# Blocks of 420 and 248 columns in a fused attention and gated MLP kernel

## The chip, the cores and the metric

The kernel runs on one core of a Trainium2 chip. The metric is the device time of one execution in microseconds (us). A core has TensorE (PE, matrix multiplies; PEld are its weight loads, which overlap with it), VectorE (DVE), ScalarE (ACT), GpSimd (POOL) and SyncE (SP), which here issues nearly all DMAs. SBUF is the memory that the engines work on, in 128 partitions; PSUM takes the results of matmuls.

## The reference

Batch 4, 4 heads, 1088 positions, head width 32. First a linear attention with products of two sketches as features, then a gated MLP whose gate mixes positions with a 1088 x 1088 matrix.

```python
def phi(x):                                   # 8 x 8 = 64 features
    a = einsum('rd,bhsd->bhsr', S1, x); b = einsum('rd,bhsd->bhsr', S2, x)
    return einsum('bhsi,bhsj->bhsij', a, b).reshape(..., 64)
kv = einsum('bhsf,bhsd->bhfd', phi(k), v); z = sum(phi(k), axis=2)
x = (einsum(phi(q), kv) / (einsum(phi(q), z) + 1e-6))      # heads side by side: 128 wide
h = gelu_tanh(x @ w_in)                       # 1024 wide
u, v = h[..., :512], h[..., 512:]
v_n = (v - mean(v)) / sqrt(var(v) + 1e-6) * g_ln
v_s = einsum('ts,bsd->btd', w_sg, v_n) + b_sg
out = x + (u * v_s) @ w_out
```

## The kernel before

**Words.** The large matmuls run in a fast fp32 form that keeps fewer bits of its operands. So each operand is split into a high and a low word (`x_h`, `x_l`, `w_h`, `w_l`, `ar[e][:, 0]` and `ar[e][:, 1]`), and a product is three matmuls: high by high, low by high, high by low. The high word is made by a cast on ScalarE, the low one by a subtraction on VectorE (or GpSimd).

**The mixing of positions** takes nearly all of the time. `w` (the transpose of w_sg) has 1088 rows, in 8 tiles of 128 and one of 64, and 1088 columns, in the three blocks of `CH`: 362, 362 and 364. v_n has 512 columns, in 4 blocks `db` of 128. One output block (db, ci) is 128 x the width of block ci.

Batch 0 computes each output block directly: 8 row tiles times three matmuls (`group`), and two more for the last tile (`tail`). For db 2 and 3 that is `standard`, for db 0 and 1 the loops near L1218 and `z0`.

Batches 1 to 3 call `pair` twice each, for db 0 and 1 (turn) and for db 2 and 3. Within `pair` the first two column blocks and the two halves of the rows (tiles 0 to 3 and 4 to 7) are a 2 x 2 matrix, which multiplies the 2 x 2 matrix of two db and two halves in the seven-product form: `product` is one of seven, 4 tiles times three matmuls of HW*2 = 362 columns. The third column block is computed plainly by `whole`. `unit` makes the u of one block (three matmuls, a Gelu on ScalarE), `evac` moves a product from PSUM and adds, `gate` multiplies by u, splits the result into words and adds its part of the output projection (three matmuls) to `po`. So the number of matmuls does not depend on the widths in `CH`.

**Combinations of w.** The seven products need sums and differences of the quarters of w. `combine` makes them once, while batch 0 is in its `standard` blocks: per row tile t (4) and half h of a block (2) it loads four pieces of w into `tmp`, forms four combinations on VectorE (three to DRAM tile `td` as words "1", "3", "2"; the fourth stays in SBUF as `t4`, three of eight slots in `t4a` and five in `t4b`). `stream` later writes one of "1", "2", "3" or the original "b" over the middle block of `w_h` and `w_l`, four times two in each batch, between products that read the old and the new words.

**Attention of the next batch** is woven between these blocks (`attention`): k1 (sketches of k, 9 matmuls), `features`, k2 (with v in `vx`, 9 tiles), kv and its words `kvt`; then for three chunks `CA` of q: q2, a round over DRAM (`dq`) that spreads the sketches into `ea` and `eb`, their product, its words in `r0` and `eb`, q3, and the division. Then v1, Gelu, LayerNorm (squares go to `waste`, a view of `kpt[2]`).

**The order** is a list written out by hand of a search, `ORDER`: one number for each step in the order in which `add` and `step` made them. Each engine runs its steps in that order, and SP is one queue for loads, stores and streams. `keep` are 12 matmuls without use that stand in the start, and 14 small ones run before the first data come (`WARM`).

**The end.** The last block is done by `finish` in two halves: scale and gate on VectorE, one fp32 matmul, addition, store.

Of the kernel before, what the change touches and what calls it, by code (L numbers as in the profile page):

```python
# [1341 lines left out]
```

## Time and profile before

| What | Value |
|---|---|
| time, median of 3 runs | 335.23 us (334.34 to 335.45) |
| the profiled execution's own time | 335.34 us |
| its span, first to last instruction | 333.2 us |
| TensorE busy | 326.9 us (98%), 2000 matmuls |
| VectorE busy | 264.8 us (79%) |
| ScalarE busy | 219.4 us (66%) |
| GpSimd busy | 54.0 us (16%) |
| DMA | 52.5 MB, 158 GB/s on average |
[...]

The span is what the profiler sees; some 2 us of the time lie around it. Durations of matmuls overlap, since one starts before the one before it has left the array, so that distances between starts tell more than durations. Idle time of an engine is time that it waits; what released it stands behind an arrow.

### The profile page before, as it was taken

To read this page: it belongs to the slowest core of one execution; us is meant where nothing else is said; L and a number is where in the kernel's file an instruction comes from. 1 tells how busy PE (TensorE), PEld (TensorE's weight loads), DVE (VectorE), ACT (ScalarE), POOL (GpSimd) and SP (SyncE) were. 2 spreads that over 40 slices of the span, in tenths; PEclk is the share of its full clock that TensorE was granted. 3 is DMA by queue.
4 is the path that set the end of the run, shared out by engine and by line. 5 is a ranking of instruction groups with operands and counts; after the bars stand their busy time and mean duration, and the time that the engine had idled before them with its cause. 6 is when DMAs were issued, how large, how long until landed. Compare 5 with 4: busy or idle time off the path is not lost.

```text
span 333.2 us, 5905 instructions
## 1 busy us (share of the span) xinstructions
PE 326.9 (98%) x2000; PEld 319.2 (96%) x2000; DVE 264.8 (79%) x603; ACT 219.4 (66%) x533; POOL 54.0 (16%) x123
## 2 busy tenths in 40 slices
PE   7999999999999999999999999999999999999995
PEld 7998899999999999999999999999999999999994
DVE  3899989999996879899786588989864595986564
ACT  6578885576899977546888964566889743233321
POOL 1695781000003300000003200000015100000000
PEclk9999999999999999999999999999999999999999
DMA  7979455656656476964458115660073038004701
GB/s 236 376 258 327 135 167 148 188 168 179 183 171 205 134 229 197 290 186 110 115 165 270 37 48 174 205 191 0 22 220 117 3 106 247 27 22 124 256 9 60
DMA packets 43854, 52.54 MB, mean 158 GB/s; under 512 B 3952, under 2 KB 41136, under 8 KB 43824
## 3 DMA queue, kind: packets, MB, share of 16 engines
q1 hardware_dynamic: 43680, 52.08, 51.0%
q8 instruction: 15, 0.25, 0.3%
q14 instruction: 15, 0.12, 0.1%
q10 hardware_dynamic: 144, 0.09, 0.1%
HBM read 43.17 MB, written 8.99 MB: 157 GB/s over the span
## 4 chain that ended last, share of the span: by engine, by line
PE 96%; DMA 1%; SPq 1%; DVE 1%; issue 0%; DVEq 0%
PE pz L830 16%; PE pz L832 16%; PE pz L831 15%; PE ps L928 4%; PE ps L747 2%; PE ps L746 2%; PE ps L745 2%; PE po L784 2%; PE po L783 2%; PE po L782 2%; PE pz L842 2%; PE pz L841 2%; PE ps L1010 2%; PE ps L920 2%; PE ps L1011 2%; PE ps L1012 2%
## 5 line engine op out<-in xcount | busy, mean ns | idle before, releaser
L830 PE MATMUL pz<-w_h,ar 128*128 128x362 f32 (+1 forms) x288 | 95.6, 332 | 0.0
L832 PE MATMUL pz<-w_l,ar 128*128 128x362 f32 (+1 forms) x288 | 94.6, 328 | 0.0
L831 PE MATMUL pz<-w_h,ar 128*128 128x362 f32 (+1 forms) x288 | 94.3, 327 | 0.0
L830 PEld LDWEIGHTS pz<-w_h,ar 128*128 128x128 f32 x288 | 54.2, 188 | 0.7
L831 PEld LDWEIGHTS pz<-w_h,ar 128*128 128x128 f32 x288 | 54.3, 188 | 0.5
L832 PEld LDWEIGHTS pz<-w_l,ar 128*128 128x128 f32 x288 | 54.2, 188 | 0.0
L776 ACT CAST gh<-gt 128x362 fp32r<-128x362 f32 (+1 forms) x47 | 22.8, 494 | 28.0 <-PE po L783 15.2
L805 ACT CAST ar<-vn 128x512 fp32r<-128x512 f32 x40 | 24.3, 618 | 17.0 <-PE pz L832 14.4
L777 DVE TENSOR_TENSOR gl<-gt,gh 128x362 fp32r<-128x362 f32 (+1 forms) x47 | 24.5, 530 | 10.3 <-ACT gh L776 9.9
L307 POOL TENSOR_TENSOR st<-st 128x4 f32<-128x4 f32 (+2 forms) x8 | 2.8, 346 | 177.7 <-DVE st L289 177.7
L806 DVE TENSOR_TENSOR ar<-vn,ar 128x512 fp32r<-128x512 f32 x40 | 27.3, 684 | 4.7 <-ACT ar L805 4.6
L751 ACT ACTIVATE u<-ps 128x362 f32<-128x362 f32 (+1 forms) x48 | 22.1, 469 | 13.0 <-PE ps L747 8.6
L324 ACT ACTIVATE vn<-vn,st 128x512 f32<-128x512 f32 x33 | 25.7, 812 | 1.7 <-POOL st L318 1.4
L775 DVE TENSOR_TENSOR gt<-gt,u 128x362 f32<-128x362 f32 (+1 forms) x47 | 24.6, 528 | 1.5 <-ACT u L751 1.2
L699 POOL TENSOR_TENSOR w_l<-w_f,w_h 128x362 fp32r<-128x362 f32 (+1 forms) x21 | 21.6, 1063 | 2.9 <-ACT w_h L652 2.6
L761 DVE SCALAR_TENSOR_TENSOR gt<-pz,g_col,b_bc 128x362 f32<-128x362 f32 (+1 forms) x31 | 18.2, 587 | 2.1 <-PE pz L842 2.1
L1022 ACT ACTIVATE kp<-vn,st 128x512 bf16<-128x512 f32 x27 | 19.4, 718 | 0.2
L1019 ACT ACTIVATE vn<-ps 128x512 f32<-128x512 f32 x27 | 16.0, 593 | 4.2 <-PE ps L1012 4.1
L782 PE MATMUL po<-gh,wout_h 128*128 128x362 f32 (+1 forms) x47 | 15.9, 339 | 0.0
L745 PE MATMUL ps<-x_h,win_h 128*128 128x362 f32 (+1 forms) x48 | 15.9, 331 | 0.0
L747 PE MATMUL ps<-x_l,win_h 128*128 128x362 f32 (+1 forms) x48 | 15.8, 329 | 0.0
L746 PE MATMUL ps<-x_h,win_l 128*128 128x362 f32 (+1 forms) x48 | 15.8, 328 | 0.0
(299 smaller groups left out, 805.3 us busy)
## 6 DMA issues: line engine op xcount, KB each, us to landing
w_l<-td SPq DMA_DIRECT2D x52, 181.0 KB, 4.6
w_h<-td SPq DMA_DIRECT2D x26, 362.0 KB, 4.4
w_f<-in_w SPq DMA_DIRECT2D x9, 544.0 KB, 6.0
tmp<-in_w SPq DMA_DIRECT2D x16, 181.0 KB, 3.4
vx<-in_v SPq DMA_DIRECT2D x8, 288.0 KB, 6.6
ea<-dq SPq DMA_DIRECT2D x12, 182.0 KB
eb<-dq SPq DMA_DIRECT2D x12, 182.0 KB, 2.9
td<-tmp SPq DMA_DIRECT2D x8, 271.5 KB
```

The lines of the kernel that those rows point to most:

```text
L324: A.activation(self.vn(t), self.vn(t), AF.Identity, bias=self.nm[:, t : t + 1], scale=self.rs[:, t : t + 1])
L745: mm(o, lhsT=win_h[:, ws], rhs=xh[:, cs], start=True, stop=False)
L746: mm(o, lhsT=win_l[:, ws], rhs=xh[:, cs], start=False, stop=False)
L775: add("V", dv(cw), lambda: V.tensor_mul(gt(k)[:, :cw], gt(k)[:, :cw], utt[plan.got[u]][:, :cw]), r=[u], w=[k], free=[u], port=1)
L776: add("A", ac(cw), lambda: A.copy(ght[plan.got[h]][:, :cw], gt(k)[:, :cw]), r=[k], take={h: "gh"})
L777: add("V", dv(cw), lambda: V.tensor_sub(glt[plan.got[l]][:, :cw], gt(k)[:, :cw], f32(ght[plan.got[h]][:, :cw])), r=[h, k], take={l: "gl"}, ...
L782: mm(o, lhsT=wout_h[:, db], rhs=hh, start=i == 1, stop=False, skip_group_check=True)
L805: add("A", ac(n), lambda: A.copy(dst[:, 0], q()), r=r, w=[key])
L806: add("V", dv(n), lambda: V.tensor_sub(dst[:, 1], q(), f32(dst[:, 0])), r=r, w=[key], port=1)
L830: mm(o, lhsT=ar[e][:, 0, t], rhs=wh, start=first, stop=False, skip_group_check=True)
L831: mm(o, lhsT=ar[e][:, 1, t], rhs=wh, start=False, stop=False, skip_group_check=True)
L832: mm(o, lhsT=ar[e][:, 0, t], rhs=wl, start=False, stop=last, skip_group_check=True)
```

## The change

- The column blocks `CH` are 420, 420 and 248 wide, `HW` is 210. Tiles that hold a block (`gt`, `u`, `gh`, `gl`) are 420 wide, `td` and the slots of `t4` too: two in `t4a`, six in `t4b`. The chunks `CA` of the attention stay.
- v of batch 0 lies in a staging tile, v of batches 1 to 3 in `ea` (first half) and `eb` (second), with a memset of its ones on GpSimd before each load. The words of kv lie in the tiles of `kp1` and `kp2`, which are made anew where they are needed; `waste` is a view of `kp0`.
- `combine` loads three times in place of two and holds the four pieces in another order, so that the three combinations that go to DRAM lie side by side: one cast for two, one subtraction for two, two stores for three.
- In the end the sums of x lie in `r0`, `ea` and `r2`.
- `ORDER` is new: 1963 steps in place of 1972.

```diff
-CH = [(0, 362), (362, 362), (724, 364)]
+CH = [(0, 420), (420, 420), (840, 248)]
-HW = 181
+HW = 210
 ORDER = [
...
 ]
-    vx = const([P, 2 * NT + 1, 64], "vx")
-    G.memset(vx[:, NT], 1.0)
...
-    kvt = [const([P, 2 * P], f"kv{i}", F32R) for i in "hl"]
...
-    waste = kpt[2].bitcast(mybir.dt.bfloat16)
+    waste = kp0.bitcast(mybir.dt.bfloat16)
...
+    vx = staged("vx", [P, 2 * NT + 1, 64], "vx")
+    step("vx1", "G", 0.1, lambda: G.memset(vx()[:, NT], 1.0))
...
-        return [t4a[0][:, 362 * i : 362 * i + 362] if i < 3 else t4b[:, i - 3] for i in (2 * t, 2 * t + 1)]
+        return [t4a[0][:, 420 * i : 420 * i + 420] if i < 2 else t4b[:, i - 2] for i in (2 * t, 2 * t + 1)]
...
+                load_(0.62, lambda t=t, c=c, s=s: load(s[:, :2], wd[:, t, : 4 * HW].rearrange("p (a c) -> p a c", a=2)[:, :, c : c + HW]), w=k[:2])
                 for i in range(2):
-                    load_(0.53, lambda t=t, i=i, c=c, s=s: load(
-                        s[:, 2 * i : 2 * i + 2], wd[:, t + 4 * i, : 4 * HW].rearrange("p (a c) -> p a c", a=2)[:, :, c : c + HW]),
-                        w=k[2 * i : 2 * i + 2])
+                    load_(0.33, lambda t=t, i=i, s=s, wp=wp: load(s[:, 2 + i], wp(t + 4, 1 - i)), w=k[2 + i : 3 + i])
...
-                add("A", ac(2 * HW), lambda s=s, hi=hi: A.copy(hi[:, :2], s[:, :2]), r=k[:2], w=hk[:2])
-                add("A", ac(HW), lambda s=s, hi=hi: A.copy(hi[:, 2], s[:, 3]), r=[k[3]], w=[hk[2]])
...
-                add("V", dv(2 * HW), port=1, f=lambda s=s, hi=hi: V.tensor_sub(f32r(s[:, :2]), s[:, :2], f32(hi[:, :2])), w=k[:2], r=hk[:2])
-                add("V", d, port=1, f=lambda s=s, hi=hi: V.tensor_sub(f32r(s[:, 3]), s[:, 3], f32(hi[:, 2])), w=[k[3]], r=[hk[2]])
...
-                load_(1.14, lambda t=t, c=c, hi=hi: load(td[:3, t, 0, :, c : c + HW].rearrange(by), f32(hi)), r=hk, w=nk[:3])
-                load_(0.8, lambda t=t, c=c, s=s: load(td[:2, t, 1, :, c : c + HW].rearrange(by), s[:, :2]), r=k[:2], w=nk[3:5])
-                load_(0.3, lambda t=t, c=c, s=s: load(td[2, t, 1, :, c : c + HW], s[:, 3]), r=[k[3]], w=nk[5:])
+                add("A", ac(3 * HW), lambda s=s, hi=hi: A.copy(hi, s[:, :3]), r=k[:3], w=hk)
+                add("V", dv(3 * HW), port=1, f=lambda s=s, hi=hi: V.tensor_sub(f32r(s[:, :3]), s[:, :3], f32(hi)), w=k[:3], r=hk)
+                for i, y, kk in ((0, f32(hi), hk), (1, s[:, :3], k[:3])):
+                    load_(1.3, lambda t=t, c=c, i=i, y=y: load(td[:3, t, i, :, c : c + HW].rearrange(by), y), r=kk, w=[("td", n, t, i, h) for n in "132"])
...
+        vh = lambda p: now["ea" if p == 0 else "eb"].rearrange("p i c -> p (i c)")[:, : 64 * NT + 64].rearrange("p (n d) -> p n d", d=64)
+
+        def ones(p):
+            here("eb" if p else "ea")
+            G.memset(vh(p)[:, 0 if p else NT], 1.0)
...
         for p in range(2):
-            load_(0.8, lambda p=p: vd_(p), w=[("vx", p)])
+            e = "eb" if p else "ea"
+            add("G", 0.12, lambda p=p: ones(p), w=[e, ("vx", p)])
+            load_(0.8, lambda p=p: vd_(p), r=[("vx", p)], w=[e])
...
-            add("PE", 0.444, k2, r=[("kp", t % 3), ("vx", 0), ("vx", 1)], w=[pkv] if t else [], take={} if t else {pkv: "ps"}, tune=at(b, "m", t))
+            add("PE", 0.444, k2, r=[("kp", t % 3), "ea", "eb"], w=[pkv] if t else [], take={} if t else {pkv: "ps"}, tune=at(b, "m", t))
...
-        add("A", ac(256), lambda: A.copy(kvt[0], kv), r=[("kp", 0)], w=["kvh"])
-        add("V", dv(256), port=1, f=lambda: V.tensor_sub(kvt[1], kv, f32(kvt[0])), r=[("kp", 0), "kvh"], w=["kvl"])
+        add("A", ac(256), lambda: A.copy(here("kp1", F32R), kv), r=[("kp", 0)], w=[("kp", 1)])
+        add("V", dv(256), port=1, f=lambda: V.tensor_sub(here("kp2", F32R), kv, f32(kpt(1))), r=[("kp", 0), ("kp", 1)], w=[("kp", 2)])
...
-            add("A", 0.72, square, r=vk, w=[mk, ("kp", 2)])
+            add("A", 0.72, square, r=vk, w=[mk, ("kp", 0)])
```

## Rows read from the trace of the kernel before

**Rows 1.** The page: busy us (share of the span); busy tenths in 40 slices.
```profile
PE 326.9 (98%) x2000; PEld 319.2 (96%) x2000; DVE 264.8 (79%) x603; ACT 219.4 (66%) x533; POOL 54.0 (16%) x123
...
PE   7999999999999999999999999999999999999995
```

**Rows 2.** The page: the chain of work that ended last, share by engine.
```profile
PE 96%; DMA 1%; SPq 1%; DVE 1%; issue 0%; DVEq 0%
```

**Rows 3.** Waits of TensorE: who waited for whom, us in total, times, longest.
```profile
PE pz L515 <- DMA vx<-in_v: 1.7, 2, 1.5
PE ps L256 <- POOL vx L218: 0.9, 1, 0.9
```

**Rows 4.** Groups by line and shape: xcount | busy us, mean ns | idle us.
```profile
L830 PE MATMUL pz<-w_h,ar 128*128 128x362 f32 x176 | 58.3, 331 | 0.0
...
L830 PE MATMUL pz<-w_h,ar 128*128 128x364 f32 x112 | 37.4, 334 | 0.0
```

**Rows 5.** Timeline of TensorE in three stretches: start us, us, engine and line.
```profile
27.88 0.39 PE L617 MATMUL ps<-win_h,x_h 128*128 128x512 f32 x1
...
32.07 1.32 PE L693 MATMUL pz<-win_h 128*128 128x512 f32 x5
...
151.95 0.33 PE L830 MATMUL pz<-w_h,ar 128*128 128x362 f32 x1
...
153.93 0.33 PE L782 MATMUL po<-gh,wout_h 128*128 128x362 f32 x1
...
151.96 0.19 PEld L831 LDWEIGHTS pz<-w_h,ar 128*128 128x128 f32 x1
```

**Rows 6.** The same timeline, short matmuls, merged: start us, us, xcount.
```profile
20.33 0.83 PE L573 MATMUL ps<-sg_ident,r 128*128 128x128 f32 x6
...
21.53 2.79 PE L557 MATMUL pz<-sg_kvx,vn 128*128 128x66 f32 x24
```

**Rows 7.** The chain that ended last, its end, in order of time.
```profile
327.49 0.42 DVE gt L1167
...
328.00 0.35 DVE gt L1168
328.35 0.33 DVE gt L1167
...
328.70 0.36 DVE gt L1168
...
329.10 0.59 PE po L1173 x2
...
329.71 0.35 DVE gt L1176
```

**Rows 8.** Groups by line and shape, VectorE.
```profile
L806 DVE TENSOR_TENSOR ar<-vn,ar 128x512 fp32r<-128x512 f32 x40 | 27.3, 684 | 4.7 <-ACT ar L805 4.6
...
L775 DVE TENSOR_TENSOR gt<-gt,u 128x362 f32<-128x362 f32 x32 | 16.9, 527 | 1.1 <-ACT u L751 0.8
...
L891 DVE TENSOR_TENSOR tmp<-tmp 128x362 fp32r<-128x362 f32 x8 | 4.2, 525 | 0.4 <-ACT tmp L888 0.3
...
L892 DVE TENSOR_TENSOR tmp<-tmp 128x181 fp32r<-128x181 f32 x8 | 3.2, 396 | 0.2
```

**Rows 9.** Busy time by stretch: PE, PEld, DVE, ACT, POOL, clock, DMA.
```profile
100.00:125.00 25.00, 25.00 (x165) 24.55 (x164) 18.58 (x49) 22.07 (x61) 6.49 (x22) 1.00 0.64 189
```

**Rows 10.** The page: DMA issues, KB each, median us from issue to landing.
```profile
w_l<-td SPq DMA_DIRECT2D x52, 181.0 KB, 4.6
w_h<-td SPq DMA_DIRECT2D x26, 362.0 KB, 4.4
...
vx<-in_v SPq DMA_DIRECT2D x8, 288.0 KB, 6.6
```

**Rows 11.** Timeline of the last stream: the issue on SP, a matmul.
```profile
309.89 0.43 SPq L902 DMA_DIRECT2D w_h<-td  x1
...
316.27 0.33 PE L830 MATMUL pz<-w_h,ar 128*128 128x362 f32 x1
```

More of the change, by code (lines that the diff above doesn't have):

```diff
@@ L244, in tile_kernel @@
     et = [x[:, i] for i in range(2) for x in (ea, eb)]
-    kpt = [const([P, 2 * P], f"kp{i}") for i in range(3)]
+    kp0 = const([P, 2 * P], "kp0")
     kbt = [const([P, 32], f"kb{i}") for i in range(2)]
-    kvt = [const([P, 2 * P], f"kv{i}", F32R) for i in "hl"]
     qld = const([P, CW], "qld")
@@ L254, in tile_kernel @@
     pst, pzt, pot = ([psum.tile([P, 512], F32, tag=f"{n}{i}", name=f"{n}{i}", bufs=1) for i in range(m)] for n, m in (("ps", 3), ("pz", 2), ("po", 3)))
+    G.memset(kp0[:, :64], 1.0)
     for i in range(WARM):
-        mm(pst[i % 3][:64, :64], lhsT=vx[:, NT], rhs=vx[:, NT], start=True, stop=True)
+        mm(pst[i % 3][:64, :64], lhsT=kp0[:, :64], rhs=kp0[:, :64], start=True, stop=True)
     def features(out, a, b):
@@ L355, in here, with kpt @@
     def here(tag, dt=F32):
-        now[tag] = swap.tile([P, 3 * P] if tag > "r0" else [P, 2, 3 * P], dt, tag=tag, name=tag)
+        now[tag] = swap.tile([P, 2 * P] if tag[0] == "k" else [P, 3 * P] if tag > "r0" else [P, 2, 3 * P], dt, tag=tag, name=tag)
         return now[tag]
+    def kpt(i):
+        return now[f"kp{i}"] if i else kp0
     def ps(k):
@@ L427, in first_loads @@
         yield "q2", (0.45, 0.18), lambda: load_q(2)
-        yield "v0", (0.88,), lambda: load(vx[:, :NT], vd[0, :, 0])
-        yield "v1", (0.75,), lambda: load(vx[:, NT + 1 :], vd[0, :, 1])
+        yield "v0", (0.88,), lambda: load(vx()[:, :NT], vd[0, :, 0])
+        yield "v1", (0.75,), lambda: load(vx()[:, NT + 1 :], vd[0, :, 1])
         yield "ident", (0.19, 0.19), lambda: [load(ident(), identd[:, :P]), load(mask, identd[:, P:])]
@@ L516, in k2_0 @@
                 pzt[1][:, P * p : P * p + P], lhsT=vn[:, t, 512 + P * p : 512 + P * p + P],
-                rhs=vx[:, NT : NT + t + 2 : t + 1] if p else vx[:, t : NT + 1 : NT - t],
+                rhs=vx()[:, NT : NT + t + 2 : t + 1] if p else vx()[:, t : NT + 1 : NT - t],
                 start=(t == 0 and p == 0), stop=(t == NT - 1 and p == 1), skip_group_check=True,
@@ L866, in combine @@
     def combine():
-        load_(2.16, lambda: load(td[3, :, 0].rearrange(by), f32(w_h[:, 4:8, 362:724])), r=[("w", t + 4, 1, 0) for t in range(4)], w=[("td", "b", t, 0) for t in range(4)])
+        load_(2.5, lambda: load(td[3, :, 0].rearrange(by), f32(w_h[:, 4:8, 420:840])), r=[("w", t + 4, 1, 0) for t in range(4)], w=[("td", "b", t, 0, h) for t in range(4) for h in range(2)])
         for t in range(4):
-            load_(0.6, lambda t=t: load(td[3, t, 1], f32(w_l[t + 4][:, 362:724])), r=[("w", t + 4, 1, 1)], w=[("td", "b", t, 1)])
+            load_(0.68, lambda t=t: load(td[3, t, 1], f32(w_l[t + 4][:, 420:840])), r=[("w", t + 4, 1, 1)], w=[("td", "b", t, 1, h) for h in range(2)])
         for t in range(4):
@@ new lines, in combine @@
+                add("V", d, port=1, f=lambda s=s: V.tensor_sub(s[:, 2], s[:, 0], s[:, 2]), w=[k[2]], r=[k[0]])
+                add("V", d, port=1, f=lambda s=s: V.scalar_tensor_tensor(s[:, 3], s[:, 2], -1.0, s[:, 3], op0=ALU.mult, op1=ALU.subtract),
+                    r=[k[2]], w=[k[3]])
+                add("A", ac(3 * HW), lambda s=s, hi=hi: A.copy(hi, s[:, :3]), r=k[:3], w=hk)
+                add("A", ac(HW), lambda s=s, th=th: A.copy(th(), s[:, 3]), r=[k[3]], w=[("t4", t)], after=[done_lo] + swapped)
@@ L901, in stream @@
             if t % 2 == 0:
-                load_(1.1, lambda t=t: load(f32(w_h[:, half + t : half + t + 2, 362:724]), TD[n][t : t + 2, 0].rearrange(by)),
-                    r=[("td", n, x, 0) for x in (t, t + 1)], w=[("w", half + x, 1, 0) for x in (t, t + 1)])
-            load_(0.53, lambda t=t: load(f32(w_l[half + t][:, 362:724]), TD[n][t, 1]), r=[("td", n, t, 1)], w=[("w", half + t, 1, 1)])
+                load_(1.28, lambda t=t: load(f32(w_h[:, half + t : half + t + 2, 420:840]), TD[n][t : t + 2, 0].rearrange(by)),
+                    r=[("td", n, x, 0, h) for x in (t, t + 1) for h in range(2)], w=[("w", half + x, 1, 0) for x in (t, t + 1)])
+            load_(0.62, lambda t=t: load(f32(w_l[half + t][:, 420:840]), TD[n][t, 1]), r=[("td", n, t, 1, h) for h in range(2)], w=[("w", half + t, 1, 1)])
     def attention(b):
@@ L923, in attention, with feat @@
             add("A", 0.09, lambda t=t, pk=pk: A.copy(kbt[t % 2], ps(pk)[:, 32:64]), r=[pk], w=[("kb", t % 2)])
-            add("V", 0.335, lambda t=t, pk=pk: features(kpt[t % 3], ps(pk)[:, :P], kbt[t % 2]), r=[pk, ("kb", t % 2)], w=[("kp", t % 3)], free=[pk])
+            def feat(t=t, pk=pk):
+                if t in (1, 2):
+                    here(f"kp{t}")
+                return features(kpt(t % 3), ps(pk)[:, :P], kbt[t % 2])
+            add("V", 0.335, feat, r=[pk, ("kb", t % 2)], w=[("kp", t % 3)], free=[pk])
             def k2(t=t):
@@ L928, in k2 @@
                     mm(
[L929 to L930 removed]
+                        ps(pkv)[:, P * p : P * p + P], lhsT=kpt(t % 3)[:, P * p : P * p + P],
+                        rhs=vh(1)[:, 0 : t + 2 : t + 1] if p else vh(0)[:, t : NT + 1 : NT - t],
                         start=(t == 0 and p == 0), stop=(t == NT - 1 and p == 1), skip_group_check=True,
                     )
[L934 to L935 removed]
+            add("PE", 0.444, k2, r=[("kp", t % 3), "ea", "eb"], w=[pkv] if t else [], take={} if t else {pkv: "ps"}, tune=at(b, "m", t))
+        kv = kp0
         add("V", 0.06 + dv(256), lambda: V.tensor_mul(
@@ L974, in q3 @@
                 def q3(pd=pd, p=p, cw=cw):
-                    o, kv = ps(pd)[:, :cw], [k[:, P * p : P * p + P] for k in kvt]
+                    o, kv = ps(pd)[:, :cw], [kpt(i)[:, P * p : P * p + P] for i in (1, 2)]
                     qp = [now[n][:, p, :cw] for n in ("r0", "eb")]
@@ L1172, in finish @@
         for i, cs in enumerate(halves(cw)):
-            pemain(pe(cw // 2) * 4, lambda cs=cs, i=i: mm(pot[ci][:, cs], lhsT=wf, rhs=gt(k)[:, cs], start=False, stop=i == 1, skip_group_check=True),
+            pemain(pe(cw // 2) * 4, lambda cs=cs, i=i: mm(pot[ci][:, cs], lhsT=wf(), rhs=gt(k)[:, cs], start=False, stop=i == 1, skip_group_check=True),
                    r=[(k, i), "wf"], w=[("po", ci), (o, i)])
@@ L1181, in xf, with wf @@
             now["x"] = here("r0")
-        return now["x"][:, ci] if ci < 2 else now["r2"]
-    wf = kpt[1][:, :C]
+        return now["r2"] if ci == 2 else now["ea" if ci else "x"].rearrange("p i c -> p (i c)")
+    def wf():
+        return kpt(1)[:, :C]
     def before_end(b):
         xh, xl = xs[b % 2]
-        add("V", dv(C), port=1, f=lambda: V.tensor_add(wf, f32(wout_h[:, NB - 1]), f32(wout_l[:, NB - 1])), r=[("wout",)], w=["wf", ("kp", 1)])
+        add("V", dv(C), port=1, f=lambda: V.tensor_add(here("kp1")[:, :C], f32(wout_h[:, NB - 1]), f32(wout_l[:, NB - 1])), r=[("wout",)], w=["wf", ("kp", 1)])
         for ci, (c0, cw) in enumerate(CH):
             add("V", dv(cw), port=1, f=lambda ci=ci, c0=c0, cw=cw: V.tensor_add(xf(ci)[:, :cw], f32(xh[:, c0 : c0 + cw]), f32(xl[:, c0 : c0 + cw])),
-                r=[("x", b % 2, c) for c in range(3)], w=[("xf", ci)] + ([("r", 2, 0), ("r", 2, 1)] if ci == 2 else ["r0"]))
+                r=[("x", b % 2, c) for c in range(3)], w=[("xf", ci)] + ([("r", 2, 0), ("r", 2, 1)] if ci == 2 else ["ea" if ci else "r0"]))
     gates = {0: g}
@@ L1301, in tile_kernel @@
     for tiles, n, name, dt in ((gtt, NG, "gt", F32), (utt, NU, "u", F32), (ght, NH, "gh", F32R), (glt, NL, "gl", F32R)):
-        tiles.extend(gp.tile([P, CW], dt, tag=f"{name}{i}", name=f"{name}{i}") for i in range(n))
+        tiles.extend(gp.tile([P, CH[0][1]], dt, tag=f"{name}{i}", name=f"{name}{i}") for i in range(n))
     with tc.manual_schedule():
```

27 lines of the change are left out of this document (10 added, 17 removed), and 165 rows, old and new, of the table ORDER.

## The prediction

> **What bounds the kernel now.** I read the table of engines and the slices of the span first: TensorE is busy 98% of the span, and over nine tenths in every slice but the first and the last [rows 1]. A busy TensorE is not yet a full one, so the chain of work that ended last comes next: 96% of it is TensorE [rows 2]. Third, the waits of TensorE: two in all, 0.9 us for the first memset and 1.7 us for the first load of v [rows 3]. After those it never waits for anybody. So from about 10 us to 327.5 us the kernel is a row of matmuls without a hole, and its time is their number times their step. Anything on VectorE, ScalarE, GpSimd or a queue costs nothing unless it opens a hole.
>
> What does a step cost? The recorded durations (331 ns for 362 columns [rows 4]) hold the way through the array and are no use; the distance between starts is. Twelve matmuls of 362 columns go from 151.95 to 153.93 us: 165 ns each. Eighteen of 512 columns go from 27.88 to 32.07 us: 232.8 ns each [rows 5]. Slope 67.8/150 = 0.452 ns a column, and 1.4 ns for a matmul. By this line 420 columns take 191.2 ns, 364 take 165.9, 248 take 113.5.
>
> **Part 1, the widths.** By the code one call of `pair` has on each of the two seven-product blocks' columns 92 matmuls in products and tails, 12 in `unit` and 12 in `gate`: 116 that go from 362 to 420 columns. On the plain rest it has 52 in `whole`, 6 and 6: 64 that go from 364 to 248. The trace confirms the count: 176 matmuls of L830 at 362 (144 of `pair`, 32 of batch 0; 24 more read the t4 words and stand apart) and 112 at 364 (96 and 16) [rows 4]. Six pairs, less the three that `finish` replaces in the last one: 696 matmuls get 58 columns more and 381 get 116 fewer. Batch 0 computes all columns without the seven products (256 and 128 matmuls), so its columns only move between blocks and cancel: 256 x 58 = 128 x 116. In columns: 40,368 - 44,196 = -3,828. At 0.452 ns that is -1.73 us, all of it on the path. This is the whole idea of the change: where seven products do the work of eight, more columns pass.
>
> The sum is good only if a 248-wide matmul really takes 113.5 ns, and no matmul of this kind between 128 and 360 columns is in the trace. The load of the weights is what could stop it. A load starts as the matmul before it starts (151.96 against 151.95 us [rows 5]). In rows of short matmuls the step does not follow the columns: 24 of 66 columns span 2.79 us, less 0.27 for the last one's own way 0.110 us each; 6 of 128 columns span 0.83 us, 0.111 us each [rows 6]. So about 110 ns is what a load takes, whatever streams. At 362 columns 55 ns of slack hide that; at 248 only 3.5 ns. Bounds for the 509 matmuls of 248 columns (381 and 128): at 110 ns another -1.8 us; at the far end the step of the nearest wider row, 165 ns, which would lose 26 us. I take 114 ns, next to the line, because a stream longer than the load should rule as it does at 362; +0.25 us.
>
> [...]
>
> **Part 2, the end.** After the last matmul of `whole` the chain is VectorE in halves, 0.42, 0.35, 0.33 and 0.36 us, then the fp32 matmuls 0.59, then the addition 0.35, then the store [rows 7]. Halves shrink from 182 to 124 columns. A VectorE column costs (684 - 527)/150 = 1.05 ns [rows 8], so five operations lose 0.06 us each: -0.30. The two passes of L1173 lose 58 columns each: -0.05. Together -0.35 us, on the path. The setup and end of the store I leave as they are.
>
> **Part 3, combinations of w.** Per quarter and half: four loads' worth of columns instead of two paired loads (three issues for two), two stores for three, two ScalarE casts for three, one VectorE subtraction of 630 columns where there were two of 362 and 181 columns. The issues on SP stay five. VectorE: 525 + 396 ns become about 527 + 268 x 1.05 = 808 ns, -0.11 us, and five operations with 29 columns more cost +0.15 us; 8 times +0.04 is +0.3 us [rows 8]. They run around 100 to 125 us, where VectorE is busy 18.6 of 25 us [rows 9]: hidden at zero. Without that cover it would be 0.3 us.
>
> **Part 4, streams of w.** Every rewrite of the middle block in `w_h` and `w_l` moves 420/362 = 1.16 times the bytes. Today 181 KB land 4.6 us after issue and 362 KB in 4.4 us [rows 10]: twice the bytes are no later, so the growth lies between 0 and 0.7 us, and I expect 0.3. The tightest place I see is the last one: its last load is issued at 309.89, lands by 314.3, and the product that starts to read rewritten words starts at 316.27 [rows 10, 11]: 2.0 us of margin. Between them stands `whole` on the plain rest, whose 26 matmuls lose 1.4 us, and about 17 at 420 columns that gain 0.4. So the margin falls to 0.3 to 1.0 us. Still hidden, at zero, but thin; the same place comes in all three batches.
>
> **Part 5, shared buffers.** v of batches 1 to 3 now lies in `ea` and `eb`, and the words of kv in `kp1` and `kp2`. So the load of v waits on SP until the last q3 of the batch before has read `eb`, and all that is queued behind it on SP (streams, q, the fills from `dq`) waits too; the first fill of `ea`/`eb` waits for the last k2, and the first q3 for that. The load takes 6.6 us to land [rows 10] and was free to go early before. GpSimd gets a memset in front of each, 6 in all, and nothing else waits for GpSimd there. The squares of LayerNorm now write into `kp0`, so ScalarE holds up feature 0 instead of feature 2. All this is off the path as long as the list orders it in time; in the list of the diff 31 TensorE steps of 88 matmuls, some 14 us at 165 ns, stand between the last projection matmul of v in batch 3 and the first product of its blocks, where 37 stood; in batches 1 and 2 more stand there than before. I take 0; bounds 0 and one load of 6.6 us for each of three batches, 20 us.
>
> **Part 6, the order.** There is no hole between 10 and 327.5 us for a better order to fill, and the 12 filler matmuls and the 14 warm-up ones stay. The order of the first loads and the place of the first k2 stay as well, so the wait for v remains [rows 3]. An order can only lose here: 0 to some us; I take +0.2 us.
>
> **Sum.** The profiled execution took 335.34 us, span 333.2 and 2.1 around it: -1.73 - 0.35 + 0.25 + 0.2 = -1.63 gives 333.7. It lies 0.1 above the median of 335.23, so the median should be **333.6 us**.
>
> **Rivals.**
> A. The weight load sets the step at 248 columns. If the load needs its 110 ns and the 0.01 us that it starts after the matmul, the step is 120 ns: 509 x 6.5 = +3.3 us, 335.23 - 2.08 + 3.3 = **336.5 us, slower**. The gain of 2.08 us is used up at 117.6 ns, and slower by 0.3% begins at 119.6. For it: 3.5 ns is all the slack there is, and the two rows of short matmuls differ by 1 ns already. Against: 0.110 us is a step start to start, so the 0.01 is probably in it. 0.14.
> B. Streamed words of w come late. From a growth of the landing of about 1.1 us on, each further us costs three batches one us each; at 2 us +2.7 us, **335.9 us**, and with a second stream in each batch caught 338. For: the margin of part 4. Against: twice the bytes land no later, and TensorE waits for no stream today. 0.12.
> C. The change does not give what it says, since the new order leaves holes of 1 to 2 us in sum at the shared buffers of part 5: **335.0 us**, no change. 0.14.
>
> **How the numbers follow.** The measurement tells about 0.3%, 1.0 us. Forecast 0.60, from 332.4 to 334.2. A splits 0.06 within 0.3% and 0.08 slower, B 0.05 and 0.07, C within. Faster 0.60, within 0.25, slower 0.15. The low end 332.4 has no hole (335.23 - 2.08 = 333.15) and some 40% of the -1.8 us of part 1; the high end 336.3 takes in C, most of B and A up to a step near 120 ns.
>
> **What would show it.** Starts of L830 at 248 columns 113 to 115 ns apart and at 420 columns 191 ns; TensorE's waits still only those of the first 10 us; the chain's end from L842 to L1176 about 2.2 us instead of 2.6. The prediction is wrong if 248-wide steps pass 118 ns, if TensorE has a wait for DMA after 100 us, or if a stretch near the first product of a pair has idle TensorE.

## The result, and the profile after

| What | Before | After |
|---|---|---|
| time, median (runs) | 334.54 us (6) | 337.70 us (6; 337.05 to 339.64) |
| the profiled execution's own time | 335.34 us | 339.64 us |
| its span | 333.2 us | 337.9 us |
| matmuls | 2000 | 2000 |
| bytes moved by DMA | 52.5 MB | 57.05 MB |

The changed kernel is slower: ratio 1.0103 with a 95% interval of 1.0069 to 1.0137, about 3.2 us. 333.6 us was predicted, with a range of 332.4 to 336.3, so both the sign and the range were missed.

First the page of the changed kernel: busy us and share of each engine, two rows of the 40 slices, and the shares of the chain that ended last. They answer to [rows 1] and [rows 2].

```profile
PE 328.3 (97%) x2000; PEld 315.9 (94%) x2000; DVE 268.6 (80%) x595; ACT 220.3 (65%) x525; POOL 55.0 (16%) x130
...
PE   7999699999999999999999999999999999999996
...
PEclk9999699999999999999999999999999999999999
...
PE 79%; DVE 8%; DMA 6%; ACT 2%; issue 1%; SPq 1%; DVEq 0%; ACTq 0%
```

TensorE is busy 97% where it was 98%, which looks like nothing. But the slice of 34 to 42 us shows a 6, with another 6 in the granted clock (its mean over the span is 0.989, and 1.000 in the kernel before), and the chain is 79% TensorE in place of 96%: VectorE, DMA and ScalarE stand in it now. So there are holes. The waits of TensorE in the changed kernel (answering to [rows 3]; us in total, times, longest):

```profile
PE ps L925 <- DMA vn<-in_k: 2.3, 1, 2.3
PE pz L516 <- DMA sg_vx<-in_v: 1.1, 2, 0.9
PE ps L746 <- DVE gt L762: 1.1, 1, 1.1
PE ps L252 <- POOL kp L250: 1.0, 1, 1.0
PE po L684 <- DVE ar L659: 0.5, 1, 0.5
...
PE pz L831 <- DVE gt L762: 0.2, 1, 0.2
```

Lines 516 and 252 are the waits of the first 10 us, which the kernel before has too. Line 925 (a sketch of k of batch 1), line 746 (a `unit`) and the two small ones are new.

**The steps themselves came out well.** The timeline of TensorE in the changed kernel (start us, us, engine, line; first and last rows of two stretches):

```profile
283.82 0.35 PE L831 MATMUL pz<-w_h,ar 128*128 128x420 f32 x1
...
286.68 0.27 PE L783 MATMUL po<-gh,wout_h 128*128 128x248 f32 x1
```

```profile
295.99 0.28 PE L831 MATMUL pz<-w_h,ar 128*128 128x248 f32 x1
...
298.71 0.28 PE L842 MATMUL pz<-w_h,rs 128*128 128x248 f32 x1
```

Fifteen matmuls of 420 columns take 2.86 us, 190.7 ns each, and twenty-four of 248 take 2.72 us, 113.3 ns each. Over all undisturbed distances between starts after 50 us the means are 190.7 (420 columns, 925 of them) and 114.3 ns (248 columns, 489), against 165.9 (362, 906) and 166.2 ns (364, 533) before.

**Where the time went.** To find the holes I took from every distance between two starts of wide matmuls what the prediction's line gives (1.4 ns + 0.452 ns a column; 110 ns for short ones), and summed what is left over by stretch, in us, for the kernel before, the changed one, and four of the experiments below:

| Stretch, us | before | after | e1_slot | e4_evac | e5_both | e8_all |
|---|---|---|---|---|---|---|
| 30 to 50 | 0.7 | 6.7 | 1.2 | 3.5 | 5.7 | 1.2 |
| 70 to 80 | 0.1 | 1.4 | 3.9 | 0.6 | 0.6 | 0.6 |
| 90 to 100 | 0.1 | 0.4 | 0.0 | 0.4 | 0.5 | 0.4 |
| 150 to 160 | 0.1 | 0.3 | 0.3 | 0.3 | 0.3 | 0.0 |
| 300 to 320 | 0.1 | 0.4 | 0.4 | 0.4 | 0.4 | 0.0 |

From 30 to 50 us it is a hole and its consequence. SP's issues of late tiles of w, and of q and k of batch 1, before and after (start us, us, line; tile<-tensor):

```profile
23.47 0.34 SPq L416 DMA_DIRECT2D w_f<-in_w  x1
...
24.42 0.60 SPq L945 DMA_DIRECT2D qld<-in_q  x1
25.12 0.68 SPq L912 DMA_DIRECT2D vn<-in_k  x1
```

```profile
27.31 0.34 SPq L416 DMA_DIRECT2D w_f<-in_w  x1
...
28.21 0.68 SPq L915 DMA_DIRECT2D vn<-in_k  x1
28.94 1.55 SPq L955 DMA_DIRECT2D qld<-in_q  x1
```

The load of tile 8 of w leaves 3.8 us later, and win0, k and q stand behind it on the queue. SP was waiting for GpSimd, as the row of the subtractions for the low words of w shows: they end at 27.29 us, and the load is issued at 27.31.

```profile
21.75 5.54 POOL L700 TENSOR_TENSOR w_l<-w_f,w_h 128x420 fp32r<-128x420 f32 x6
```

The pool `w` has ten buffers, given out in the order in which the list comes to the tiles. In the old list tile 8 got the buffer of tile 2. In the new one the low words of tile 4 come ahead of tile 8 and take that buffer, and tile 8 gets the buffer of tile 3, which is free only when GpSimd has done three more subtractions. The kernel before had no room for this: by the last of the 16 semaphore updates of its load, k landed there at 34.60 us, and its first use starts at 34.73. TensorE then finds k missing, and a little later a slower clock. The timeline of TensorE, and busy time by stretch (PE, PEld, DVE, ACT, POOL, granted clock, DMA share, GB/s), both of the changed kernel:

```profile
36.50 0.68 PE L925 MATMUL ps<-sk,vn 128*128 128x128 f32 x4 [2.25 <-DMA vn<-in_k]
```

```profile
30.00:34.00 4.00, 4.00 (x19) 3.18 (x17) 3.72 (x12) 3.73 (x10) 3.02 (x4) 1.00 0.97 319
34.00:36.50 2.50, 0.25 (x3) 0.03 (x1) 0.74 (x3) 0.38 (x2) 1.60 (x7) 1.00 1.10 361
...
37.00:43.90 6.90, 6.19 (x22) 5.24 (x21) 6.04 (x13) 4.52 (x14) 4.55 (x11) 0.51 0.22 66
43.90:60.00 16.10, 16.10 (x109) 15.84 (x109) 14.30 (x29) 11.39 (x26) 6.66 (x12) 1.00 0.41 124
```

TensorE stands still from 34.25 to 36.50 us, and from 37.0 to 43.9 us the granted clock is 0.51; from 30 to 37.0 us and from 43.9 to 60 us it is 1.00.

The second hole is on VectorE's account. The timelines of VectorE and TensorE in the changed kernel:

```profile
71.98 0.38 DVE L884 TENSOR_TENSOR tmp<-tmp 128x210 f32<-128x210 f32 x1 [2.42 <-DMA tmp<-in_w]
```

```profile
76.65 0.46 PE L746 MATMUL ps<-x_h,win_h 128*128 128x420 f32 x1 [1.05 <-DVE gt L762]
```

VectorE stands 2.4 us at a subtraction of the third combination of w, whose load lands at 71.9 us. The evacuation that frees a PSUM bank (L762) stands behind it, and TensorE waits 1.05 us for that bank.

**What the prediction named as signs.** Of its three signs of being wrong, two did not come (steps of 248 columns past 118 ns, a wait of TensorE for DMA after 100 us), and the third is small: 0.2 us idle before a product at 311 us. What failed is the sign that TensorE's waits would still be only those of the first 10 us: the holes are at 34 and 75 us. The end, from `scale` to the addition (answering to [rows 7]):

```profile
...
333.09 0.36 DVE gt L1177
333.47 0.29 DVE gt L1178
333.76 0.27 DVE gt L1177
334.05 0.30 DVE gt L1178
334.40 0.50 PE po L1183 x2
334.92 0.29 DVE gt L1186
```

From 333.09 to 335.21 us it takes 2.12 us, in place of 2.57. The combined subtraction of the combinations and the first of their four small ones (groups by line, xcount | busy us, mean ns | idle us and releaser; answering to [rows 8]):

```profile
L891 DVE TENSOR_TENSOR tmp<-tmp 128x630 fp32r<-128x630 f32 x8 | 6.5, 807 | 0.6 <-ACT tmp L889 0.6
...
L884 DVE TENSOR_TENSOR tmp<-tmp 128x210 f32<-128x210 f32 x8 | 3.0, 370 | 2.4 <-DMA tmp<-in_w 2.4
```

### The profile page after: what moved, and what is told of

It reads as the page before. It is cut to its first block, busy times and chain, and to the rows that moved or that the text cites. A ratio compares the mean times of both kernels' runs of the same rounds, so it can differ in the third digit from the quotient of the medians.

```text
span 337.9 us, 5893 instructions
## 1 busy us (share of the span) xinstructions
PE 328.3 (97%) x2000; PEld 315.9 (94%) x2000; DVE 268.6 (80%) x595; ACT 220.3 (65%) x525; POOL 55.0 (16%) x130
## 2 busy tenths in 40 slices
DMA packets 43853, 57.05 MB, mean 169 GB/s; under 512 B 4208, under 2 KB 41136, under 8 KB 43824
## 4 chain that ended last, share of the span: by engine, by line
PE 79%; DVE 8%; DMA 6%; ACT 2%; issue 1%; SPq 1%; DVEq 0%; ACTq 0%
PE pz L831 14%; PE pz L832 14%; PE pz L833 14%; PE ps L938 4%; DMA qld<-in_q 2%; PE po L784 2%; PE po L785 2%; PE po L783 2%; PE pz L842 2%; PE pz L843 2%; PE ps L925 2%; PE ps L746 2%; PE ps L748 2%; DMA tmp<-in_w 2%; PE ps L747 2%; PE ps L1020 2%
## 5 line engine op out<-in xcount | busy, mean ns | idle before, releaser
L831 PE MATMUL pz<-w_h,ar 128*128 128x420 f32 (+1 forms) x288 | 94.2, 327 | 0.2 <-DVE gt L762 0.2
L832 PE MATMUL pz<-w_h,ar 128*128 128x420 f32 (+1 forms) x288 | 93.1, 323 | 0.0
L833 PE MATMUL pz<-w_l,ar 128*128 128x420 f32 (+1 forms) x288 | 93.0, 323 | 0.0
L777 ACT CAST gh<-gt 128x420 fp32r<-128x420 f32 (+1 forms) x47 | 23.0, 494 | 17.0 <-DVE gt L776 13.0
L752 ACT ACTIVATE u<-ps 128x420 f32<-128x420 f32 (+1 forms) x48 | 22.4, 468 | 14.5 <-DVE gt L776 6.7
L778 DVE TENSOR_TENSOR gl<-gt,gh 128x420 fp32r<-128x420 f32 (+1 forms) x47 | 24.7, 531 | 6.4 <-ACT gh L777 6.3
L776 DVE TENSOR_TENSOR gt<-gt,u 128x420 f32<-128x420 f32 (+1 forms) x47 | 24.7, 530 | 0.2
L700 POOL TENSOR_TENSOR w_l<-w_f,w_h 128x420 fp32r<-128x420 f32 (+1 forms) x21 | 23.3, 1139 | 6.2 <-ACT w_h L653 6.0
L762 DVE SCALAR_TENSOR_TENSOR gt<-pz,g_col,b_bc 128x420 f32<-128x420 f32 (+1 forms) x31 | 17.8, 573 | 6.5 <-PE pz L843 4.2
L746 PE MATMUL ps<-x_h,win_h 128*128 128x420 f32 (+1 forms) x48 | 16.1, 335 | 1.1 <-DVE gt L762 1.1
L747 PE MATMUL ps<-x_h,win_l 128*128 128x420 f32 (+1 forms) x48 | 15.7, 328 | 0.0
```

Source lines behind the costliest of these rows:

```text
L700: return G.tensor_sub(w_l[t][:, cs], w_f[t][:, cs], f32(w_h[:, t, cs]))
L746: mm(o, lhsT=win_h[:, ws], rhs=xh[:, cs], start=True, stop=False)
L747: mm(o, lhsT=win_l[:, ws], rhs=xh[:, cs], start=False, stop=False)
L776: add("V", dv(cw), lambda: V.tensor_mul(gt(k)[:, :cw], gt(k)[:, :cw], utt[plan.got[u]][:, :cw]), r=[u], w=[k], free=[u], port=1)
L777: add("A", ac(cw), lambda: A.copy(ght[plan.got[h]][:, :cw], gt(k)[:, :cw]), r=[k], take={h: "gh"})
L778: add("V", dv(cw), lambda: V.tensor_sub(glt[plan.got[l]][:, :cw], gt(k)[:, :cw], f32(ght[plan.got[h]][:, :cw])), r=[h, k], take={l: "gl"}, ...
```

## The experiments

Each has a label, of which e1, e2 and so on are short forms. Ratios are to the kernel before on the same chip. Its medians there were 334.88 us beside the unedited kernel, e1, e2 and e3, 334.86 beside e4, e5, e6 and e8, and 334.73 beside e9, e10 and e11. "Full clock" is a mean granted clock of 0.997 or more in an execution.

**The changed kernel again,** with no line edited.

> The changed kernel once more, as the measure for the three beside it. Theory: what was lost lies in two places of the new list (a hole of 2.3 us at 34 us, where TensorE waits for k of batch 1, and one of 1.1 us at 75 us), so they stand again at the same two places, and the time is 337.0 to 338.5 us. Rival: the loss was chance of one run; then the holes are gone or elsewhere and the time is below 336.

338.59 us, ratio 1.0090 (1.0063 to 1.0116), 0.1 us above the range expected. The profiled execution has holes in the same two stretches, but the one at the start is of another kind. Only 0.6 us is lost at line 925 at 34 us, and 2.1 us at the same line at 39.8 us, where TensorE waits for a feature on VectorE. Its wait, the first of three small instructions on VectorE ahead of that feature, and GpSimd at that time; below them the same instruction in the profiled execution of e2:

```profile
PE ps L925 <- DVE kp L257: 1.9, 1, 1.9
```

```profile
38.92 1.04 DVE L281 TENSOR_SCALAR st<-st 128x3 f32<-128x3 f32 x1
```

```profile
38.76 2.87 POOL L700 TENSOR_TENSOR w_l<-w_f,w_h 128x420 fp32r<-128x420 f32 x3
```

```profile
39.38 0.16 DVE L281 TENSOR_SCALAR st<-st 128x3 f32<-128x3 f32 x1
```

The three instructions (lines 281, 284 and 285, three columns each) take 1.04, 1.00 and 0.63 us here, while GpSimd subtracts for the low words of w. In the eight profiled executions where the two do not meet, e2 among them, they take 0.15 to 0.17 us each; in e3, e4, e10 and e11, where they meet, one or two of them take 0.7 to 1.0 us. No run was made for this loss alone. The chain of work behind it comes from the load of q, which stands right behind k on the queue and lands at 35.1 us. So the start loses in two ways: k comes late, or VectorE, behind q, meets GpSimd. Of the six profiled executions that leave the start as it is (the changed kernel twice, e2, e3, e4 and e10) only that of e2 loses little from 30 to 50 us (1.2 us).

**One buffer (e1).** In `ORDER`, one number moves nine places:

```diff
+    40,
     267,
...
-    40,
     41,
```

> Only the entry of the load of w's tile 8 stands nine places earlier in the list, ahead of the first subtraction that makes tile 4 of the low words of w. No engine's order changes; only the buffer that tile 8 gets is another (that of tile 2 instead of tile 3). Theory: this load waits on SP for GpSimd to have done with tile 3, at 27.3 us, and win0, k and q of batch 1 stand behind it; with tile 2's buffer it leaves 3 us earlier, k lands by about 33.5 instead of 36.4, the hole at 34 us closes, and the time falls by 2 to 3 us to about 335.0. Rival: the DMA engines are full in this stretch (k took 8.2 us to land), so k lands as late as before: 337.2 or more, with the hole still over 1.5 us.

336.69 us, ratio 1.0056 (1.0029 to 1.0084): 1.9 us gained on the unedited kernel beside it, less than expected. SP's timeline, and TensorE's longest wait:

```profile
24.46 0.34 SPq L433 DMA_DIRECT2D w_f<-in_w  x1
...
25.42 0.68 SPq L932 DMA_DIRECT2D vn<-in_k  x1
```

```profile
PE ps L763 <- DVE gt L779: 2.1, 1, 2.1
```

The load leaves 2.9 us earlier, and the wait for k is gone: 30 to 50 us loses 1.2 us in place of 6.7. But now the hole at the `unit` is 2.1 us (line 763 here is line 746 there), since TensorE comes there 5.0 us earlier, and VectorE, whose load of w lands at 68.0 in place of 71.9 us, only 4.0 us. It brings a lower clock of its own, 0.50 from 72.6 to 76.0 us. Expected was the gain; that it would be given back at the next place was not.

**The list's two parts (e2).** The steps are recorded in two parts, split where the staging space is given back, and the program did not keep the list's order across the split: the two first subtractions of the second part came to stand five VectorE instructions early, ahead of work that was ready.

```diff
-    cut = 1 + max(seq.index(i) for i in staging)
+    cut = 5 + max(seq.index(i) for i in staging)
```

> The list is recorded in two parts, and the first two subtractions of the third of the eight combinations begin the second part; in the recorded program they stand five VectorE instructions earlier than the list has them. Here the first part is four entries longer, so they stand where the list has them; on SP one of two fills of ea goes ahead of one load of w for it. Theory: VectorE stands still for 2.4 us at 69.5 us because it meets a subtraction whose load lands at 71.9; with five other instructions first that is gone, the PSUM bank that TensorE waits for at 75.6 is read earlier, and the time falls by 1.0 to 1.3 us to about 336.4. Rival: VectorE is full around there and reads the bank as late, or the combinations' other steps come later and the wait shows up a few us on: 337.5.

336.2 us, ratio 1.0048 (1.0027 to 1.0069). The time is near the expected one, but it is 2.4 us below the unedited kernel beside it, twice the gain expected, and the run looked at doesn't show the mechanism. (Nine of its twelve executions, and two of those six, are at full clock.) VectorE's stand there shrinks from 2.42 to 1.35 us, and TensorE waits as long as before:

```profile
70.67 0.38 DVE L884 TENSOR_TENSOR tmp<-tmp 128x210 f32<-128x210 f32 x1 [1.35 <-DMA tmp<-in_w]
```

```profile
PE ps L746 <- DVE gt L762: 1.0, 1, 1.0
```

In that run the start happened to lose only 1.2 us between 30 and 50, so TensorE came early, as in the experiment above. Where the gain comes from stays open. The subtractions still stood ahead of the evacuation. So their place in front of it, not the five instructions, was what to change.

**The evacuation first (e4).** In the list, three subtractions (632 to 634) go behind the evacuation (402):

```diff
-    632,
...
-    633,
...
-    634,
     402,
+    632,
+    633,
+    634,
     373,
```

> Three subtractions of the third combination of w stand behind the evacuation of PSUM that TensorE waits for at 75 us, in place of ahead of it; nothing else moves. Theory: the evacuation was late because it stood on VectorE behind subtractions whose load lands late, so the hole at 75 us (1.2 us, and 1.1 still where those subtractions stood later) closes to under 0.4, and since the hole at 34 us is left as it is, the time falls by about 1.2 us, to 336 to 337.5. Rival: VectorE as a whole is too full from 60 to 75 us; then the evacuation comes as late, or the hole shows up again up to 90 us, and the time stays at 337.5 or more.

336.94 us, ratio 1.0055 (1.0024 to 1.0087). The hole at 75 us closes (0.6 us lost between 70 and 80 in place of 1.4), and no wait for an evacuation is left among the large ones. The start still loses 3.5 us, 1.6 of it where VectorE meets GpSimd:

```profile
PE ps L942 <- DVE kp L274: 1.4, 1, 1.4
...
PE ps L942 <- DMA vn<-in_k: 0.3, 1, 0.3
```

**Both (e5)**, the edits of e1 and e4 together, with no other line changed.

> Both edits: the earlier place of the load of w's tile 8, and the evacuation ahead of the three subtractions. Theory: with the first alone, the time won at 34 us was given back at 75 us, where the wait grew from 1.2 to 2.3 us because TensorE came there earlier and VectorE's load did not; so together they give more than the sum, no hole over 0.5 us is left after 10 us, the granted clock stays at 1.00, and the time is 334.2 to 335.4. Rival: the time won moves on to a third place behind 75 us, and the time stays at 336 or more.

334.46 us, ratio 0.9993 (0.9963 to 1.0023): each edit alone left some 2 us over the kernel before, and together they leave nothing. But that no hole stays was wrong for some executions. Three of the twelve took 335.9 to 338.5 us, the profiled one among them: there TensorE waits for k again, and the granted clock is lower from 37.7 to 41.1 us (its mean over the span is 0.995).

```profile
PE ps L942 <- DMA vn<-in_k: 2.0, 1, 2.0
```

So the rival of e1, that the DMA engines are full here, holds in part: their share is 0.97 to 1.10 from 30 to 36.5 us in the rows by stretch above. When k was issued and when it landed in the profiled executions (last of the 16 updates of its semaphore), in us:

| | before | after | again | e1 | e4 | e5 | e9 | e8 | e11 |
|---|---|---|---|---|---|---|---|---|---|
| issued | 25.1 | 28.2 | 28.0 | 25.4 | 28.3 | 26.7 | 25.8 | 25.4 | 28.5 |
| landed | 34.6 | 36.4 | 34.6 | 34.2 | 34.9 | 36.5 | 33.5 | 32.4 | 36.2 |

It takes 6.5 to 9.8 us, and three us of lead at the issue do not always come out at the landing. In e9 and e8, where tile 7 too leaves earlier, it takes 7.7 and 7.0 us, against 8.8 and 9.8 us in e1 and e5; so what is ahead of k on the engines, tile 7, w_out, tile 8 and win0, may count as well.

**Tile 7 too (e9).** The entry of the load of tile 7 also goes ahead, and it takes the buffer of tile 0:

```diff
+    36,
     263,
...
-    36,
     37,
```

> The evacuation ahead of the three subtractions, and earlier buffers for both late tiles of w, 7 and 8; none of the three swaps of neighbours. Theory: what made the start uneven with tile 8 alone (a hole of 2.15 us in the run looked at, where k took 9.7 us to land) is that tile 7, w_out, tile 8 and win0 are all moved just ahead of k; with tile 7 loaded 3 us earlier the queue ahead of k is shorter, no run shows a lower clock, and the time is 334.0 to 334.6, some 0.8 us (the three swaps) above the kernel with all edits. Rival: the swaps made the difference and tile 7 does nothing; then single runs of 336 to 338 us stay among these, with a median of 334.5 or more.

333.49 us, ratio 0.9976 (0.9952 to 1.0001). Tile 7 leaves at 18.9 us where it left at 22.5, k lands by 33.5 us, and the median falls by 1.0 us; by the ratios it is 0.2%, and their intervals overlap, so what tile 7 is worth isn't settled by the times. Two of twelve executions show a clock of 0.993 and 0.995 (337.0 and 335.1 us), and "no run" was expected. But the one of 335.1 us is the profiled one, which has no hole over 0.4 us after 12 us. Its clock falls at 329.8 us, after the last matmul (328.6), and what stands behind that matmul, the addition and the stores, takes 4.7 us, where it takes 3.0 us in e8 (and 4.5 us in e2). So a mean clock below full does not always mean a hole. The median is lower than expected by 0.5 us.

**All edits (e8)**, with three swaps in the list: on TensorE a tail (717) ahead of a q3 (512), on ScalarE a copy out of PSUM (1019) ahead of a Gelu (1058), on VectorE an evacuation (1870) ahead of a subtraction (1840):

```diff
-    512,
...
     717,
+    512,
...
+    1019,
     1058,
...
-    1019,
...
+    1870,
     1840,
...
-    1870,
```

> Both edits, and four more: the load of w's tile 7 also takes an earlier buffer, and three small waits of 0.3 us each are taken away by swapping neighbours (at 96 us a tail goes ahead of a q3, at 157 us a copy on ScalarE goes ahead of a Gelu, at 311 us an evacuation goes ahead of a subtraction). Theory: no hole is left between 10 and 327 us, so the time is that of the steps: the kernel before less 1.7 us for the widths, 333.0 to 334.0. Rival: with both big holes closed the start is bound by the DMA engines, which moves a hole of 1 us or more to another place: 335 or more.

333.49 us (332.65 to 334.77), ratio 0.9947 (0.9924 to 0.9970): faster than the kernel before by 0.5%, and every one of ten executions below 334.8. The span of the profiled one is 331.4 us. All of TensorE's waits:

```profile
PE ps L269 <- POOL kp L267: 1.0, 1, 1.0
PE ps L529 <- DMA k<-in_k: 0.5, 1, 0.5
PE ps L763 <- ACT u L769: 0.2, 1, 0.2
```

The medians of this run and the last are the same, on different occasions, and the intervals of their ratios overlap, so what the three swaps are worth (0.7 us by the table above) isn't shown by the times.

**The buffer, put into the kernel before (e11).** The same edit the other way round, in the list of the kernel before:

```diff
-    39,
...
     266,
+    39,
```

> The kernel before, with the entry of the load of w's tile 8 moved 29 places later in its list, so that it takes the buffer of tile 3, as in the changed kernel; no engine's order changes. Theory: the load waits for GpSimd until 26.7 us instead of 23.5, q and k of batch 1 behind it land 3 us later (k at 37.7 where TensorE wants it at 34.8), and the kernel before gets a hole of 2 us or more at 35 us: 336.5 to 338.5. Rival: the hole in the changed kernel is made by its other early loads, not by this buffer; then this stays at 334.9.

336.37 us, ratio 1.0047 (1.0022 to 1.0071). The wait for k is there, in a kernel that had no hole after 10 us; tile 8 was issued at 27.11 us in place of 23.47:

```profile
PE ps L936 <- DMA vn<-in_k: 1.9, 1, 1.9
```

So that one buffer alone makes the hole, and costs the kernel before 1.6 us; 1.8 to 3.8 were expected. The clock is lower here too, from 37.5 to 40.9 us (its mean over the span is 0.993).

**Work in the hole (e10),** ten matmuls ahead of the first sketch of k:

```diff
+                for _ in range(10 if (b, t) == (1, 0) else 0):
+                    mm(ps(pk), lhsT=win_h[:, DG : DG + P], rhs=win_h[:, DG:], start=True, stop=True)
                 mm(ps(pk)[:, :P], lhsT=vn[:, t, ...], rhs=sk, start=True, stop=True)
```

> The changed kernel with ten matmuls of 512 columns, without use, ahead of the first sketch of k of batch 1, where TensorE stood still for 2.3 us: 2.3 us of work into the same PSUM bank. [...]

337.47 us, ratio 1.0088 (1.0064 to 1.0113). That is ten matmuls more and 0.7 us less than the median of the twelve executions of the unedited kernel. But the unedited kernel has ratios of 1.0090 and 1.0103 to the kernel before on the same chip, so the times show no gain clear of noise. What differs is the clock: all six have a mean clock of 0.998 or more, where seven of those twelve had 0.995 or less. The stretches that answer to those of the changed kernel:

```profile
34.00:37.00 3.00, 1.69 (x9) 1.42 (x9) 1.22 (x4) 1.17 (x6) 2.21 (x9) 1.00 1.01 351
37.00:44.00 7.00, 6.57 (x46) 6.05 (x44) 6.03 (x16) 5.04 (x15) 5.83 (x15) 1.00 0.29 85
```

Of the hole at k 1.3 us are left, and the clock stays at 1.00. A median of about 337 us was expected for that case; it came out 0.5 us above it, and one execution of 339.0 us stands out, at full clock. With the same loads on the same queue, DMA engines as busy (a share of 1.01 from 30 to 37 us, where it is 0.97 to 1.10 in the changed kernel) and less standstill (1.3 us in place of 2.25) the clock did not fall. That speaks for the standstill as what brings it down, and not the traffic; it rests on one profiled execution and six mean clocks.

**The old widths in the new list (e3),** with the slices of the middle block moved likewise:

```diff
-CH = [(0, 420), (420, 420), (840, 248)]
+CH = [(0, 362), (362, 362), (724, 364)]
-HW = 210
+HW = 181
```

> The changed kernel, list and buffers as they are, with the old widths of 362, 362 and 364 columns. Theory: the widths alone are worth what the steps say, 1.7 to 2.1 us, and the loss comes from the list; so this is the slowest of all, 339 to 340 us, with both holes still there. Rival: the widths are what costs, by more bytes in each rewrite of w and by weight loads that no longer hide; then this comes near the kernel before, 334.5 to 336 us.

344.27 us, ratio 1.0267 (1.0243 to 1.0291): 5.7 us above the changed kernel, more than expected. The steps explain about half of it (2.8 us by the means above). Most of the rest is waits that the new list has at the old widths: from 80 to 320 us its distances are 5.9 us over the line, where those of the kernel before and of the changed one are 1.2 us over it; 1.6 us of that is made up for before 80 us, where it loses less than c1_after_again. The two largest:

```profile
PE pz L831 <- DVE gt L762: 0.7, 1, 0.7
PE po L785 <- DVE gl L778: 0.5, 1, 0.5
```

So the widths are not what costs, and this list fits the widths that it was searched for.

**The old list on the new buffers (e6).** The list of the kernel before, with new steps at the place of the old ones, and what the buffers forbid put off:

```diff
 ORDER = [
-    1, 11, 12, 13, 14, 15, 16, 17, 18, 50, 2, 3, 4, 0, 5, 6, 7, 51, 42, 49, 48, 43, 52, 45,
+    1, 0, 2, 3, 11, 4, 5, 6, 7, 8, 12, 13, 14, 15, 16, 17, 18, 48, 9, 49,
...
 ]
```

> The changed kernel (widths, buffers, combinations) with the list of the kernel before: every step at its old place, and where that cannot be, because the shared buffers are still in use, right behind the step that frees them (25 of 1963 steps, among them the load of v of batch 2 about 200 entries later and the second fill of ea and eb in batch 2 by 180). Theory: the new buffers, which I had costed at nothing, take away the old list's order in batches 2 and 3, so that TensorE waits there at q3 and the projections, 5 us or more in sum, 338.5 or more. Rival: the buffers cost nothing and the new list is the whole of the loss; then this is 333.3 to 334.5, the time that the widths promised.

378.27 us, ratio 1.1278 (1.1230 to 1.1327). TensorE's waits and the first of VectorE's:

```profile
PE pz L859 <- DVE rs L1080: 10.9, 1, 10.9
PE ps L1004 <- ACT kp L966: 8.7, 1, 8.7
```

```profile
DVE ea L995 <- DMA eb<-dq: 15.3, 2, 7.8
```

VectorE waits 15.3 us in two places for the fills of `eb`, and TensorE 10.9 and 8.7 us behind it: these fills came long before their use in the old list, and now they must stand behind v and k2. So the old list, with its steps put off in this way, takes 43 us more on the new buffers, with a clock that falls three times in the profiled execution (its mean over the span is 0.964); what another way of putting them off would cost isn't shown. In the new list TensorE waits for none of them; that list made them free, and in it are the two holes.

## Why the prediction was wrong

*Part 1, the widths: right, and better than said.* Neither bound came near: at 248 columns the mean step is 114.3 ns, where the line has 113.5, so the load of the weights, 110 ns by the prediction's estimate, does not set it. The matmuls at steady steps give 952 x 24.8 = +23.6 us and 509 x 51.9 = -26.4 us, so -2.8 us; -1.5 was said (-1.73 and 0.25). The line through twelve and eighteen matmuls gave 165.0 ns for 362 columns, where the mean of 906 is 165.9, and 191.2 for 420, where it is 190.7: 1.4 ns on a thousand matmuls. In columns the counting of the prediction stands. Rival A is out.

*Part 2, the end: right.* 0.45 us for 0.35.

*Part 3, the combinations: the operations right, the cover wrong.* The subtraction of 630 columns takes 807 ns; 808 was said. But "they run around 100 to 125 us" was read off one stretch. In the kernel before they are loaded from 35.8 us on, in the changed one from 30.6, and at 70 us VectorE, standing at one of them, holds up TensorE. What was hidden was the work; the wait for its load was never costed.

*Part 4, the streams: right.* TensorE waits for no stream in any run with the new list and widths. Rival B is out.

*Part 5, the shared buffers: right in value, wrong in the reason.* TensorE doesn't wait for them. But my ground was that enough entries of TensorE stand in between, which is the work of the new list, and what that list loses elsewhere I didn't look for. The buffers that cost were others, the ten of `w`, which the diff touches through the list alone.

*Part 6, the order: the step that failed.* "An order can only lose here: 0 to some us; I take +0.2 us" has the right sign; the size was 5 us at full clock, and near 7 with the clock. Two grounds for the 0.2 failed. The first loads were said to stay in their order: on SP they do as far as win0 (behind it q and k of batch 1 change places), but which buffer a load takes is settled by the whole list, GpSimd's entries too, and with it the time at which it can leave. And the kernel before was read as if no hole meant room. In the execution profiled its k lands 0.13 us ahead of its use, so a longer delay of k is a hole. Part 4 worked out such a margin for the last stream; the same reading at the start would have found this one.

*Rival C* had the kind (holes from the new list, 1 to 2 us in sum) and the wrong place and size. Its price left out that in some executions a lower clock comes on top of the hole: of the twelve executions of the changed kernel, the five at full clock have a median of 337.05 us, the seven below it one of 338.91, 1.9 us more. Holes of other lengths and a slower end, as in e9, can be in that difference too; the matmuls at the lower clock alone account for 1.5 us or more, as the last section shows.

The sum of what was measured: -2.8 for the steps, -0.45 for the end, +2.8 for the start at full clock (30 to 50 us in e4, 3.5 less 0.7, of which 1.6 where VectorE meets GpSimd), +1.3 at 75 us and +0.9 for the three small waits give +1.8 us; the executions at full clock lie 2.5 us above the kernel before, and the 0.7 between is open: the start, and the time behind the last matmul, differ from run to run. With the holes closed the time is 333.5 us. That it meets the number predicted is in part chance: the prediction started from 335.23 us, 0.4 to 0.7 us above the medians of the kernel before that were found later, the steps gain 1.3 us more than the sum had, and 1.3 us of small waits remain over the kernel before (0.5 between 30 and 50 us, 0.5 from 70 to 80, 0.3 from 90 to 100).

## What to carry to other kernels

A new order is a change of its own. Before costing it at nothing, list what each early load waits for, its buffer above all, and how many tenths of a us lie between each landing and its use; a rotating pool gives buffers out in the order of the whole program, so an entry of one engine moves another engine's load. A hole mended in one place gives its time to the next, so mend them together before judging either. And if a list is recorded in parts, compare the program with it at the seams.
